# Convolution of an H3 block beside attention: one channel or two in each strip of 32 PSUM rows

## The chip, the core and the metric

The kernel runs on one core of one Trainium2 chip. The core has five engines that run side by side and meet only at semaphores: TensorE (PE: matrix products, with its weight loads shown as PEld), VectorE (DVE), ScalarE (ACT), GpSimd (POOL) and SyncE (SP, which here only issues DMA transfers). Matrix products end in PSUM, which has 128 rows (partitions) and 8 banks of 512 fp32 columns. The metric is the device time of one execution in microseconds (us).

## The reference

Two blocks are computed independently and their outputs stand side by side in the last dimension. S is 2048, D is 512, all tensors are bf16.

```python
# block A: attention, 32 heads of 16
q, k, v = split(x @ wqkv)
a = softmax(q @ k.T * 16 ** -0.5) @ v        # per head
a = merge_heads(a) @ wo
# block B: a short and a long causal convolution per channel
kv = shift_conv(k, shift_k) * v              # 4 taps along S
y = long_conv(kv, ssm_k) + kv * ssm_D        # filter as long as S, per channel
b = q * y
out = concatenate([a, b], -1)                # (1, 2048, 1024)
```

The reference does the long convolution with FFTs. The kernel does it directly, as matrix products with a Toeplitz matrix of each channel's filter.

## The kernel before

**Attention sets the pace.** The 2048 x 2048 scores of 32 heads are cut into 2048 blocks of 128 keys x 512 queries. A step (number `T`) handles 2 or 3 blocks: `emit_qk` (L776) issues the score products into as many PSUM banks, ACT takes the exponential of all of them in one instruction (L794) of 1024 or 1536 columns into the ring `PT`, and two steps later `emit_pv` multiplies by the values (L862). In part of the steps with three blocks one block is not given to ACT: `exp_on_dve` (L808) computes it on DVE in four passes (L813, L822 twice, L823), with one linear pass on POOL (L289) between the first and the second. So a block can be moved from ACT to DVE, which makes one ACT instruction 1024 columns instead of 1536 and adds four DVE passes.

**The convolution fills PE's gaps.** Time is cut into 16 blocks of 128 (`NB` is 16). For a channel, output block t is the sum over lags n of a 128 x 128 Toeplitz matrix times input block t - n. The tile `KV` (`[128, channel/4, block, channel%4]`) holds the gated input, blocks in reverse order. For a lag, the stationary operand is `KV` of one channel, blocks n to 15 (16 - n columns), and the moving operand is 128 columns of the channel's filter windows `WR`. Four channels run at once, one in each strip of 32 PSUM rows (`tile_position=(0, 32 * c)`), and such a group of four is a `qd`: 128 of them, each with 16 lags, 8192 matmuls in all (`conv_lags`, L977 to L1006, the matmul at L988). A channel's result fills rows 0 to 15 of its strip and 128 columns of the bank `BGB`; rows 16 to 31 stay unused. Four `qd`s fill the bank's 512 columns, then DVE copies the bank to one half of `YB` (L1004), which frees the bank. When both halves are full, `conv_turn` (L1009) transposes them with eight matmuls (L1015) into a bank of the attention's ring, and one DVE product with the gate `QN` (L1030) gives 32 finished channels. So 32 copies and 16 turns are made.

**The filter's way.** `kz_turn` (L625) reverses the 512 filter rows into `KZS`, four neighbouring channels in each partition. `kz_store` (L630) writes `KZS` to the scratch `kz_scratch` in HBM with one DMA, row d of the scratch being channel d. `load_wr` (L965) then reads for row d, 128 times overlapping, `128 x 2048` windows into a ring of 14 slots, on SP's queue; the first loads wait for the store. Behind the store on SP's queue stand loads of `B_v` and `B_k` for the gated input (`load_kv`, L418).

**What sets the order.** Each engine executes in order, and that order is made when the program is built: the code keeps its own estimate of each engine's clock (`Eng.t`, `Mm`). `commit_one` (L292) picks the next DVE job by its due time. `form` (L1246) decides at each step whether a third block goes to DVE, by the DVE work that is still open (`DVE_OPEN`), and whether a side task (`next_unit`: projections, a turn, an output product) takes the third bank. `emit_lags` (L1124) puts convolution lags into the time that PE has before the next scores are due, and stops at a new bank fill while `BGB` isn't free. `keep_active` (L1102) adds products with zeros to an open sum where little PE work is planned. A change of any job's count therefore rearranges the program.

Of the kernel before, what the change touches and what calls it, by code (L numbers as in the profile page):

```python
# [24 lines left out]
C = 512  # L25
NB = S // 128
# [145 lines left out]
def bass_concat_heads__mha_block__ssm_conv_h3__prompt_kernel(  # L172
# [24 lines left out]
    def sb(name, shape, dt=BF16):  # L197
        return enter(nc.sbuf_tensor(name, shape, dt))
# [5 lines left out]
    VAF = sb("VAF", [128, KT, VROW])  # L204
    PT = sb("PT", [128, R_PT, 3 * QB])
    WR = sb("WR", [128, R_W, S])
    KV = sb("KV", [128, C // 4, NB, 4])
    QN = sb("QN", [128, NB, 256])
    WQ = sb("WQ", [128, 4, D])
    MSK = sb("MSK", [128, 2, 4], FP32)  # L210
# [10 lines left out]
    EI = sb("EI", [128, 4, QB], INT32)  # L221
    EM = sb("EM", [128, 2, QB], FP32)
    ZER = sb("ZER", [128, 128])
    XL = KV[:, :, :, :].rearrange("p q t r -> p (q t r)").rearrange("p (t d) -> p t d", t=NB)
    XH = EI[:, :, :].rearrange("p i f -> p (i f)").bitcast(BF16).rearrange("p (t d) -> p t d", t=8)

    def xn(t):
# [130 lines left out]
    def full(n, k):  # L358
        return [("full", 0, n)] * k

    def dma(eng, dsem, outp, inp, deps=(), transpose=False):
        h = dsem.add()

        def fn(e):
            f = e.dma_start_transpose if transpose else e.dma_start
            f(outp, inp).then_inc(dsem.sem, 16)  # L366
        eng.op(fn, deps, inc=False)
        return h
# [89 lines left out]
    vones = VAF[:, :, 0:H * VW].rearrange("p k (h e) -> p k h e", e=VW)  # L458
    pool.op(lambda e: e.memset(vones[:, :, :, DH:VW], 1.0))
    h_vaf1 = pool.op(lambda e: e.memset(VAF[:, :, H * VW:VROW], 1.0))  # L460
    h_zer = pool.op(lambda e: e.memset(ZER[:, :], 0.0))
    h_kz0 = pool.op(lambda e: e.memset(KZS[:, :, S:S + PAD], 0.0))
    pool.op(lambda e: e.wait_ge(*h_xn[3]), inc=False)
# [165 lines left out]

    def kz_store():  # L630
        h = dve_op(lambda e: e.tensor_tensor(KZS[:, :, S - 1:S], KZS[:, :, S - 1:S], DSS, ALU.add), [h_kzt[0]], 100.0)
        h_kzw[0] = dma(sp, d_kzw, kz_ap.rearrange("(p c) m -> p c m", c=4), KZS, [h, h_kz0])

    kv_pieces += [lambda c=c: kz_turn(c) for c in range(4)] + [lambda: (kz_store(), load_kv(5, h_kzt[0]))]
    for j in range(7, -1, -1):
# [326 lines left out]
    h_wr, h_wrfree, h_qn = {}, {}, {}  # L962
    h_yb, h_yb_in = {}, {}

    def load_wr(d, deps=()):  # L965
        r = d % R_W
        deps = [h_kzw[0], *deps] if d < R_W else [h_wrfree[d - R_W]]
        if d < R_W:
            line[0] += 1350.0
        src = bass.AP(tensor=kz_ap.tensor, offset=kz_ap[d, 0].offset, ap=[[1, 128], [1, S]])  # L970
        h_wr[d] = dma(sp, d_wr[r], WR[:, r, :], src, deps)
# [3 lines left out]
                      q2[128 * t0:128 * t1, 256 * i:256 * i + 256].rearrange("(t p) d -> p t d", p=128), deps)  # L975

    def conv_lags(qd, n0, n1):  # L977
        kk = qd % 8
        deps = [h_wr[4 * qd + c] for c in range(4)] + [h_kvc[0]]
        if kk % 4 == 0 and n0 == 0:  # L980
            deps.append(bank_free[BGB])

        def fn(e):
            ins = None
            for n in range(n0, n1):
                for c in range(4):
                    d = 4 * qd + c
                    ins = e.matmul(PS[32 * c:32 * c + NB - n, BGB, 128 * (kk % 4):128 * (kk % 4) + 128],  # L988
                                   lhsT=KV[:, qd, n:NB, c],
                                   rhs=WR[:, d % R_W, 128 * (NB - 1 - n):128 * (NB - n)],  # L990
                                   start=(n == 0), stop=(n == NB - 1), tile_position=(0, 32 * c))
            return ins
        h = pe_op(fn, deps, [("col", c, 128) for n in range(n0, n1) for c in range(4)])
        if n1 == NB:
            for c in range(4):
                h_wrfree[4 * qd + c] = h
                if 4 * qd + c + R_W < C:
                    load_wr(4 * qd + c + R_W)
            if kk % 4 == 3:
                half = kk // 4  # L1000
                src = PS[:, BGB, :]
                src = bass.AP(tensor=src.tensor, offset=PS[:, BGB, 127:128].offset,
                              ap=[src.ap[0], [128, 4], [-1, 128]])
                bank_free[BGB] = dve_job(lambda e: e.tensor_copy(YB[:, half, :].rearrange("p (k i) -> p k i", k=4), src),  # L1004
                                         [h, (lambda: h_yb.get(qd // 8 - 1, WAIT)) if qd >= 8 else None])
                h_yb_in[qd // 4] = bank_free[BGB]  # L1006
        return h

    def conv_turn(b, bank, slack):  # L1009
        pbf = PS[:, bank, :].bitcast(BF16)  # L1010

        def fn(e):
            ins = None
            for k in range(8):
                ins = e.transpose(pbf[:, 128 * k:128 * k + 128], YB[:, k // 4, 128 * (k % 4):128 * (k % 4) + 128],  # L1015
                                  IDN[:, :])
            return ins
        h = pe_op(fn, [bank_free[bank], h_yb_in[2 * b], h_yb_in[2 * b + 1], h_idn], full(128, 8))
        h_yb[b] = h
        sl = b // 8  # L1020
        yv = pbf.rearrange("p (c j) -> p c j", j=32)[:, :, 0:NB].rearrange("p c j -> p j c")
        yv = bass.AP(tensor=yv.tensor, offset=pbf[:, NB - 1:NB].offset, ap=[yv.ap[0], [-1, NB], [32, CHB]])
        qv = QN[:, :, CHB * (b % 8):CHB * (b % 8) + CHB]

        def store(hh):
            dst = out2[:, D + 256 * sl:D + 256 * (sl + 1)].rearrange("(t p) c -> p t c", p=128)
            ho = dma(pool, d_outB[0], dst, QN[:, :, :], [hh])
            if sl == 0:
                dve_later.append((len(chunks) + 14, lambda: load_qn(1, [ho], 0, NB)))
        bank_free[bank] = dve_job(lambda e: e.tensor_tensor(qv, yv, qv, ALU.mult), [h, lambda: h_qn.get(sl, WAIT)],  # L1030
                                  slack=slack, then=store if b % 8 == 7 else None)
# [26 lines left out]
    def next_unit(T):  # L1058
        st = state
        found = []  # L1060
        if st["u"] < len(units):
            n, u = units[st["u"]]
            free = st["started"] and flow["nxt"] >= 4 * KT * (int(n) - 2 * NG + 2) if n >= NG else True
            if free and steps_to(n) < 40:
                found.append((steps_to(n) - 16, "u", u))
        if st["turn"] > st["turned"] and at_job(h_yb_in[2 * st["turned"] + 1]) + 45.0 <= pe.t:
            found.append((4.0 - st["qd"] % 4 * 4 + 8, "turn", st["turned"]))
        if st["op"] < len(later_op) and at_job(h_otn.get(later_op[st["op"]][0] * 4 + 3, WAIT)) + 45.0 <= pe.t:
            u = later_op[st["op"]]
            found.append((steps_to((u[0] + 2) * NG) - 40, "op", u))  # L1070
        return min(found, key=lambda x: x[0]) if found else None
# [52 lines left out]
    def emit_lags(T):  # L1124
        st = state
        if T in tail_mm:
            assert st["qd"] == C // 4 and st["turned"] == C // 32 and st["op"] == len(later_op), (T, st)
            for t, j in tail_mm[T]:
                op_mm(NQB - 1, t, j, j + 1, tail_banks[t])
            keep_tail(T)  # L1130
            return
        if st["qd"] == C // 4:
            if flow["NT"] is None or T < flow["NT"] - 12:
                bank_free[BGB] = pe_op(keep_busy, [bank_free[BGB]], full(512, 2))
            else:
                keep_tail(T)
            return
        if not st["started"]:
            fill(max(max(Mm.tile), pe.t), at_of(h_exp[T]) - PE_SLACK)
            st["now"] = at_of(h_exp[T])  # L1140
            return
        limit = at_of(h_exp[T]) - PE_SLACK
        now = at_of(h_exp[T])
        ahead = [(st["wr"][i] + 1500.0 - now) / (NB * (i - st["qd"]) - st["lag"]) for i in range(st["qd"] + 1, len(st["wr"]))]
        st["lags"] = min(st["lags"] + (now - st["now"]) / max([PACE] + ahead), 2.0 * LAGS)
        st["now"] = now
        lags = LAGS
        while st["qd"] < C // 4:
            t = max(max(Mm.tile), pe.t)
            advance(t)  # L1150
            n0 = st["lag"]
            if n0 == 0 and (st["wr"][st["qd"]] + 1000.0 > t or st["qd"] % 4 == 0 and at_job(bank_free[BGB]) > t):
                if st["qd"] % 4 == 0 and lags == LAGS:
                    fill(t, limit)
                break
            k = min(lags, int(st["lags"]), NB - n0, int((limit - t) / LAG_NS))
            if k < 1:
                break
            lags -= k
            st["lags"] -= k  # L1160
            conv_lags(st["qd"], n0, n0 + k)
            st["lag"] = (n0 + k) % NB
            if n0 + k == NB:
                st["qd"] += 1
                st["dma"] = max(st["dma"], max(Mm.tile) + 2500.0) + DMA_NS
                st["wr"].append(st["dma"])
                st["turn"] = st["qd"] // 8
# [227 lines left out]
```

## Time and profile before

| | us |
|---|---|
| median of 3 runs (lowest, highest) | 847.8 (844.84, 854.87) |
| the profiled execution, its own time | 846.45 |
| its span in the profile | 844.7 |
| ACT, DVE, PE busy | 820.3, 799.2, 714.4 |

The span runs from the first to the last instruction that the profile shows; the rest of the profiled execution's time, 1.75 us, lies around it. In the views an instruction is named by its line, its engine, its operation and its tiles. PE's busy time overlaps with itself (several matmuls in flight), so its sum says little of how full PE is; ACT and DVE execute one after the other, and their busy shares can be read as they stand.

### The profile page before, as it was taken

How to read it: one execution, taken by the hardware profiler on the slowest of the kernel's cores; microseconds unless marked ns; L12 is line 12 of the kernel's file. 1: busy time of each engine (PE TensorE's matmuls, PEld its weight loads, DVE VectorE, ACT ScalarE, POOL GpSimd, SP SyncE). 2: the span in 40 equal slices, each digit the busy share in tenths (PEclk: the TensorE clock that was granted, in tenths of full speed). 3: DMA queues.
4: the chain of work that ended last, by engine and by line, in shares of the span. 5: the costliest groups of instructions: out<-in, count | busy, mean ns of one | idle time of the engine just before them, and what ended most of it. 6: DMA issues, size and time to landing. Idle time of an engine off the chain costs nothing.

```text
span 844.7 us, 30021 instructions
## 1 busy us (share of the span) xinstructions
PE 714.4 (85%) x13191; PEld 308.0 (36%) x13238; DVE 799.2 (95%) x1346; ACT 820.3 (97%) x732; POOL 287.9 (34%) x318
## 2 busy tenths in 40 slices
PE   8988888888888888888888888888788888888897
PEld 3322333433344333343333333333334433334332
DVE  3998899999999999999999999999999999999996
ACT  6998999999999999999999999999999999999997
POOL 3232233333433333333333423333333333333331
PEclk9999999999999999999999999999999999999999
DMA  9978699999999999999999999999999999999810
GB/s 314 314 255 298 211 410 343 370 408 402 391 375 371 373 410 365 390 385 390 365 376 365 321 408 407 408 374 373 357 378 390 363 400 404 364 381 396 320 52 25
DMA packets 88435, 295.69 MB, mean 350 GB/s; under 512 B 11125, under 2 KB 19314, under 8 KB 87922
## 3 DMA queue, kind: packets, MB, share of 16 engines
q1 hardware_dynamic: 82386, 280.00, 87.6%
q0 software_dynamic: 3776, 12.58, 4.4%
q8 instruction: 105, 1.72, 0.8%
q10 hardware_dynamic: 2144, 1.18, 0.5%
q14 instruction: 24, 0.20, 0.1%
HBM read 287.31 MB, written 6.42 MB: 348 GB/s over the span
## 4 chain that ended last, share of the span: by engine, by line
ACT 59%; DVE 25%; PE 9%; issue 2%; DMA 2%; POOL 1%; SPq 1%; ACTq 0%; DVEq 0%
ACT PT L794 59%; DVE PTD L823 5%; DVE EI L813 5%; DVE EM L822 5%; DVE WKV L822 4%; PE PS L787 3%; PE PS L862 2%; DMA WR<-in_B_ssm_D_dram 2%; SPq L366 1%; DVE DT L888 1%; PE PS L988 1%; DVE YB L1004 1%; DVE QT L540 1%; PE PS L936 1%; DVE OUTA L948 1%
## 5 line engine op out<-in xcount | busy, mean ns | idle before, releaser
L794 ACT ACTIVATE PT<-PS 128x1024 bf16<-128x1024 f32 (+1 forms) x726 | 816.7, 1337 | 12.9 <-PE PS L787 11.1
L787 PE MATMUL PS<-QT,KTo 32*128 32x512 bf16 x2048 | 287.9, 385 | 110.4 <-ACT PT L794 91.2
L988 PE MATMUL PS<-WR,KV 128*7 128x128 bf16 (+15 forms) x8192 | 252.8, 220 | 3.4 <-issue 3.2
L289 POOL TENSOR_SCALAR EM<-EI 128x512 f32<-128x512 uint16 x129 | 125.2, 970 | 235.6 <-DVE WKV L822 104.1
L988 PEld LDWEIGHTS PS<-WR,KV 128*7 128x7 bf16 (+15 forms) x8192 | 169.5, 87 | 83.7 <-issue 42.4
L289 POOL TENSOR_SCALAR WKV<-EI 128x512 f32<-128x512 uint16 x128 | 125.0, 977 | 199.9 <-DVE EM L822 86.1
L862 PE MATMUL PS<-PT,VAF 128*32 128x512 bf16 x1791 | 187.8, 392 | 2.0 <-issue 0.8
L813 DVE TENSOR_SCALAR EI<-PS 128x512 int32<-128x512 f32 x257 | 176.0, 685 | 4.1 <-PE PS L787 3.9
L822 DVE SCALAR_TENSOR_TENSOR EM<-EM 128x512 f32<-128x512 f32 x258 | 173.9, 686 | 2.7 <-POOL EM L289 2.5
L787 PEld LDWEIGHTS PS<-QT,KTo 32*128 32x128 bf16 x2048 | 72.0, 91 | 273.2 <-ACT PT L794 213.4
L822 DVE SCALAR_TENSOR_TENSOR WKV<-WKV 128x512 f32<-128x512 f32 x256 | 170.7, 689 | 0.5 <-POOL WKV L289 0.4
L823 DVE SCALAR_TENSOR_TENSOR PTD<-EI,EM 128x512 uint16<-128x512 int32 x129 | 88.6, 689 | 0.4
L823 DVE SCALAR_TENSOR_TENSOR PTD<-EI,WKV 128x512 uint16<-128x512 int32 x128 | 87.5, 687 | 0.4
L862 PEld LDWEIGHTS PS<-PT,VAF 128*32 128x32 bf16 x1791 | 47.6, 93 | 108.2 <-issue 97.3
L862 PE MATMUL PS<-PTD,VAF 128*32 128x512 bf16 x257 | 79.3, 389 | 0.4
L1112 PE MATMUL PS<-IDN,ZER 128*32 128x512 bf16 x424 | 46.6, 381 | 0.1
L888 DVE STREAM_TRANSPOSE DT<-PS 128x512 f32<-128x512 f32 x31 | 22.2, 716 | 7.5 <-PE PS L862 7.0
L862 PEld LDWEIGHTS PS<-PTD,VAF 128*32 128x32 bf16 x257 | 19.8, 95 | 17.4 <-DVE PTD L823 6.7
L540 DVE TENSOR_TENSOR QT<-PS,MSK 128x1024 bf16<-128x1024 f32 x15 | 18.4, 1224 | 4.5 <-PE PS L505 4.3
L1004 DVE CAST YB<-PS 128x512 bf16<-128x512 f32 x32 | 22.0, 687 | 0.4 <-PE PS L988 0.2
L366 POOL DMA_DIRECT2D WR<-in_B_k_dram x15 | 11.0, 741 | 23.3 <-DVE KV L616 14.8
L519 PE MATMUL PS<-WKV,xT 128*128 128x512 bf16 x58 | 17.8, 383 | 1.0 <-issue 0.8
(79 smaller groups left out, 292.6 us busy)
## 6 DMA issues: line engine op xcount, KB each, us to landing
WR<-kz_scratch SPq DMA_DIRECT2D x512, 512.0 KB, 8.0
WR<-in_B_k_dram POOLq DMA_DIRECT2D x15, 256.0 KB, 7.6
kz_scratch<-WR SPq DMA_DIRECT2D x1, 2176.0 KB, 8.6
out_dram<-QN POOLq DMA_DIRECT2D x2, 1024.0 KB, 8.0
QT<-in_B_k_dram POOLq DMA_DIRECT2D x7, 256.0 KB, 8.8
out_dram<-OUTA POOLq DMA_DIRECT2D x12, 128.0 KB, 6.4
WR<-in_B_v_dram SPq DMA_DIRECT2D x5, 256.0 KB, 9.1
WR<-in_B_k_dram SPq DMA_DIRECT2D x5, 256.0 KB, 10.6
```

What stands on the lines that cost most here:

```text
L289: q.h = pool.op(lambda e: e.tensor_scalar(UB[m % len(UB)], f, PA, PB, ALU.mult, ALU.add), [h, fx.h, free], cost=Beside((h[0], h[1] + 1)))
L540: hh = dve_job(lambda e: e.tensor_tensor(QT[:, qb % 2, 2 * o:2 * o + 2, :], src, MSK[:, :, 0:1].broadcast_to([128, 2, QB]), ALU.mult), [h, ...
L787: ins = e.matmul(PS[:, bank, :], lhsT=KTo[32 * s:32 * s + 32, g // 2, kt * 128:(kt + 1) * 128], rhs=QT[32 * s:32 * s + 32, qb % 2, g, :], ...
L794: h_exp[T] = act.op(lambda e: e.activation(PT[:, T % R_PT, 0:n * QB], PS[:, banks[0]:banks[0] + n, :].rearrange("p b f -> p (b f)"), ACT.E ...
L813: h_fix[i] = job(lambda e: e.tensor_scalar(ei, PS[:, bank, :], FIX_LO, FIX_ADD, ALU.max, ALU.add), [h, h_pair.get(i - 4)], 692.0, end)
L822: js.append(job(lambda e, c=c: e.scalar_tensor_tensor(u, u, c, u, ALU.add, ALU.mult), [js[-1]], 693.0, due + 700.0 * (len(js) - 3)))
L823: js.append(job(lambda e: e.scalar_tensor_tensor(PTD[:, i % 4, :].bitcast(UINT16), ei, 2.0 ** -9, u, ALU.mult, ALU.add), [js[2], (lambda: ...
L862: ins = e.matmul(PS[32 * s:32 * s + 32, pvb(qb * NG + g), :], lhsT=VAF[:, kt, h * VW:h * VW + 32], rhs=rhs, start=first[b], stop=last[b], ...
L888: h_t = dve_job(lambda e: e.transpose(out=dt, in_=PS[:, pvb(n), :]), [h, h_mult.get(n - 2 if n == 2 else n - 1) if n != 1 else None], 717. ...
L988: ins = e.matmul(PS[32 * c:32 * c + NB - n, BGB, 128 * (kk % 4):128 * (kk % 4) + 128], lhsT=KV[:, qd, n:NB, c], rhs=WR[:, d % R_W, 128 * ( ...
L1004: bank_free[BGB] = dve_job(lambda e: e.tensor_copy(YB[:, half, :].rearrange("p (k i) -> p k i", k=4), src), [h, (lambda: h_yb.get(qd // 8 ...
L1112: ins = e.matmul(PS[32 * s:32 * s + 32, pvb(n), :], lhsT=ZER[:, 0:32], rhs=IDN[:, :].rearrange("p (a f) -> p a f", a=1).broadcast_to([128, ...
```

## The change

Two channels share a strip: one in rows 16 to 31, the other in rows 0 to 15. The strip's first channel gets a stationary operand of 32 - n columns: the channel's own blocks and, ahead of them, the 16 blocks that lie before them in the tile, those of the channel four lower (for the first channels, 64 columns of zeros, which are added to the tile, now `KVP`, and set by POOL). Its product puts the channel's result into rows 16 to 31 and unwanted sums into rows 0 to 15. Then the second channel's products, 16 - n columns as before, start afresh in rows 0 to 15 and overwrite these. So eight `qd`s fill a bank where four did; a bank holds 32 channels; `YB`'s halves become two whole buffers, and a turn takes four transposes of one of them. `chan(d)` says which channel the d-th filter row belongs to, and `kz_store` writes the rows to the scratch in that order, with four DMAs (one for each of the four rows of a partition), so that `load_wr` still reads row d of the scratch.

```diff
-    KV = sb("KV", [128, C // 4, NB, 4])
+    KVP = sb("KVP", [128, 4 * NB + C * NB])
+    KV = KVP[:, 4 * NB:4 * NB + C * NB].rearrange("p (q t r) -> p q t r", t=NB, r=4)
...
+    h_kvp = pool.op(lambda e: e.memset(KVP[:, 0:4 * NB], 0.0))
...
     def kz_store():
...
-        h_kzw[0] = dma(sp, d_kzw, kz_ap.rearrange("(p c) m -> p c m", c=4), KZS, [h, h_kz0])
+        rows = kz_ap.rearrange("(o e h j) m -> o h e j m", e=2, h=2, j=2)
+        for i in range(4):
+            h_kzw[0] = dma(sp, d_kzw, rows[:, :, 1 - i % 2, i // 2, :], KZS[:, i, :], [h, h_kz0])
...
+    def chan(d):
+        return 8 * (d // 8) + 2 * (d % 4) + 1 - d % 8 // 4
...
     def conv_lags(qd, n0, n1):
-        kk = qd % 8
-        deps = [h_wr[4 * qd + c] for c in range(4)] + [h_kvc[0]]
-        if kk % 4 == 0 and n0 == 0:
+        kk = qd // 2 % 4
+        m = 2 - qd % 2
+        deps = [h_wr[4 * qd + c] for c in range(4)] + [h_kvc[0], h_kvp]
+        if qd % 8 == 0 and n0 == 0:
             deps.append(bank_free[BGB])
...
-                    ins = e.matmul(PS[32 * c:32 * c + NB - n, BGB, 128 * (kk % 4):128 * (kk % 4) + 128],
-                                   lhsT=KV[:, qd, n:NB, c],
+                    ch = chan(d)
+                    o = 4 * NB * (ch // 4 + 2 - m) + 4 * n + ch % 4
+                    ins = e.matmul(PS[32 * c:32 * c + m * NB - n, BGB, 128 * kk:128 * kk + 128],
+                                   lhsT=KVP[:, o:o + 4 * (m * NB - n) - 3:4],
                                    rhs=WR[:, d % R_W, 128 * (NB - 1 - n):128 * (NB - n)],
                                    start=(n == 0), stop=(n == NB - 1), tile_position=(0, 32 * c))
...
-            if kk % 4 == 3:
-                half = kk // 4
+            if qd % 8 == 7:
+                half = qd // 8 % 2
...
     def conv_turn(b, bank, slack):
...
-            for k in range(8):
-                ins = e.transpose(pbf[:, 128 * k:128 * k + 128], YB[:, k // 4, 128 * (k % 4):128 * (k % 4) + 128],
-                                  IDN[:, :])
+            for k in range(4):
+                ins = e.transpose(pbf[:, 128 * k:128 * k + 128], YB[:, b % 2, 128 * k:128 * k + 128], IDN[:, :])
...
-        yv = bass.AP(tensor=yv.tensor, offset=pbf[:, NB - 1:NB].offset, ap=[yv.ap[0], [-1, NB], [32, CHB]])
+        yv = bass.AP(tensor=pbf.tensor, offset=pbf[:, NB - 1:NB].offset, ap=[pbf.ap[0], [-1, NB], [NB, CHB]])
```

The remaining lines follow from these: `next_unit` asks for one full buffer instead of two halves, and `emit_lags` treats every eighth `qd` as a new bank fill instead of every fourth.

More of the change, by code (lines that the diff above doesn't have):

```diff
@@ L223, in bass_concat_heads__mha_block__ssm_conv_h3__prompt_kernel @@
     ZER = sb("ZER", [128, 128])
-    XL = KV[:, :, :, :].rearrange("p q t r -> p (q t r)").rearrange("p (t d) -> p t d", t=NB)
+    XL = KVP[:, 4 * NB:4 * NB + C * NB].rearrange("p (t d) -> p t d", t=NB)
     XH = EI[:, :, :].rearrange("p i f -> p (i f)").bitcast(BF16).rearrange("p (t d) -> p t d", t=8)
@@ L1004, in conv_lags @@
                 bank_free[BGB] = dve_job(lambda e: e.tensor_copy(YB[:, half, :].rearrange("p (k i) -> p k i", k=4), src),
-                                         [h, (lambda: h_yb.get(qd // 8 - 1, WAIT)) if qd >= 8 else None])
-                h_yb_in[qd // 4] = bank_free[BGB]
+                                         [h, (lambda: h_yb.get(qd // 8 - 2, WAIT)) if qd >= 16 else None])
+                h_yb_in[qd // 8] = bank_free[BGB]
         return h
@@ L1013, in fn @@
             ins = None
-            for k in range(8):
-                ins = e.transpose(pbf[:, 128 * k:128 * k + 128], YB[:, k // 4, 128 * (k % 4):128 * (k % 4) + 128],
-                                  IDN[:, :])
+            for k in range(4):
+                ins = e.transpose(pbf[:, 128 * k:128 * k + 128], YB[:, b % 2, 128 * k:128 * k + 128], IDN[:, :])
             return ins
-        h = pe_op(fn, [bank_free[bank], h_yb_in[2 * b], h_yb_in[2 * b + 1], h_idn], full(128, 8))
+        h = pe_op(fn, [bank_free[bank], h_yb_in[b], h_idn], full(128, 4))
         h_yb[b] = h
         sl = b // 8
-        yv = pbf.rearrange("p (c j) -> p c j", j=32)[:, :, 0:NB].rearrange("p c j -> p j c")
-        yv = bass.AP(tensor=yv.tensor, offset=pbf[:, NB - 1:NB].offset, ap=[yv.ap[0], [-1, NB], [32, CHB]])
+        yv = bass.AP(tensor=pbf.tensor, offset=pbf[:, NB - 1:NB].offset, ap=[pbf.ap[0], [-1, NB], [NB, CHB]])
         qv = QN[:, :, CHB * (b % 8):CHB * (b % 8) + CHB]
@@ L1065, in next_unit @@
                 found.append((steps_to(n) - 16, "u", u))
-        if st["turn"] > st["turned"] and at_job(h_yb_in[2 * st["turned"] + 1]) + 45.0 <= pe.t:
-            found.append((4.0 - st["qd"] % 4 * 4 + 8, "turn", st["turned"]))
+        if st["turn"] > st["turned"] and at_job(h_yb_in[st["turned"]]) + 45.0 <= pe.t:
+            found.append((12.0 - st["qd"] % 8 * 2, "turn", st["turned"]))
         if st["op"] < len(later_op) and at_job(h_otn.get(later_op[st["op"]][0] * 4 + 3, WAIT)) + 45.0 <= pe.t:
@@ L1151, in emit_lags @@
             n0 = st["lag"]
-            if n0 == 0 and (st["wr"][st["qd"]] + 1000.0 > t or st["qd"] % 4 == 0 and at_job(bank_free[BGB]) > t):
-                if st["qd"] % 4 == 0 and lags == LAGS:
+            if n0 == 0 and (st["wr"][st["qd"]] + 1000.0 > t or st["qd"] % 8 == 0 and at_job(bank_free[BGB]) > t):
+                if st["qd"] % 8 == 0 and lags == LAGS:
                     fill(t, limit)
```

## The prediction

> **What bounds the kernel now.** I read the page first (busy times, then the chain that ended last), then the groups of instructions with shapes kept apart, then the waits, and last the order in time around the filter's store and around one piece of the convolution.
>
> ```profile
> span 844.7 us, 30021 instructions
> PE 714.4 (85%) x13191; PEld 308.0 (36%) x13238; DVE 799.2 (95%) x1346; ACT 820.3 (97%) x732; POOL 287.9 (34%) x318
> ...
> ACT 59%; DVE 25%; PE 9%; issue 2%; DMA 2%; POOL 1%; SPq 1%; ACTq 0%; DVEq 0%
> ACT PT L794 59%; DVE PTD L823 5%; DVE EI L813 5%; DVE EM L822 5%; DVE WKV L822 4%; PE PS L787 3%; PE PS L862 2%; DMA WR<-in_B_ssm_D_dram 2%; SPq L366 1%; DVE DT L888 1%; PE PS L988 1%; DVE YB L1004 1%; DVE QT L540 1%; PE PS L936 1%; DVE OUTA L948 1%
> ```
>
> ACT is busy for 97% of the span and DVE for 95%. The chain runs through ACT for 59% and through DVE for 25%: the two share the exponentials and are loaded about equally. PE's share of the chain is 9%. So a change on PE counts only where it makes ACT wait, and work taken from DVE counts by what it takes off ACT.
>
> ```profile
> L794 ACT ACTIVATE PT<-PS 128x1536 bf16<-128x1536 f32 x339 | 518.3, 1577 | 5.2 <-PE PS L787 4.6
> L794 ACT ACTIVATE PT<-PS 128x1024 bf16<-128x1024 f32 x387 | 422.1, 1128 | 7.8 <-PE PS L787 6.5
> L813 DVE TENSOR_SCALAR EI<-PS 128x512 int32<-128x512 f32 x257 | 176.0, 685 | 4.1 <-PE PS L787 3.9
> L822 DVE SCALAR_TENSOR_TENSOR EM<-EM 128x512 f32<-128x512 f32 x258 | 173.9, 686 | 2.7 <-POOL EM L289 2.5
> L823 DVE SCALAR_TENSOR_TENSOR PTD<-EI,EM 128x512 uint16<-128x512 int32 x129 | 88.6, 689 | 0.4
> L1004 DVE CAST YB<-PS 128x512 bf16<-128x512 f32 x32 | 22.0, 687 | 0.4 <-PE PS L988 0.2
> ...
> L1015 PE MATMUL PS<-IDN,YB 128*128 128x128 bf16 x128 | 9.9, 220 | 0.4 <-DVE EI L813 0.4
> ```
>
> These rows (busy total, mean of one, idle time before) price both engines. ACT waits 5.2 + 7.8 = 13.0 us in all between its exponentials, little beside 844.7. A block of 512 columns that leaves an ACT instruction of 1536 makes it one of 1024: by busy time 518.3/339 - 422.1/387 = 1529 - 1091 = 438 ns, by the mean durations 1577 - 1128 = 449 ns. The same block on DVE is four passes of 685, 686, 686 and 689 ns, 2.75 us.
>
> ```profile
> PEld PS L787 <- ACT PT L794: 213.4, 448, 2.3
> PE PS L787 <- ACT PT L794: 91.2, 212, 2.1
> ACT PT L794 <- PE PS L787: 11.1, 24, 1.3
> POOL WR L366 <- DMA EI<-in_A_x_dram: 8.5, 1, 8.5
> ```
>
> In the waits (total us, times, longest) PE stands before the score products because ACT hasn't freed their banks: the matmuls 212 times for 91.2 us, 0.43 us each, their weight loads for 213.4 us. The reverse happens 24 times for 11.1 us.
>
> **Copies on DVE.** 16 of the 32 copies of the bank go. Their price is 16 x 687 ns = 11.0 us of DVE. The time isn't left free: the build order of the changed program has 261 blocks on DVE instead of 257, and on ACT 391 instructions of 1024 columns and 335 of 1536, still 726. Four more blocks cost DVE 4 x 2.75 = 11.0 us, exactly what was freed. DVE therefore comes out level, and ACT loses 4 x 0.438 = 1.75 us (1.80 by the other price). POOL gets four linear passes more, and is idle most of the time (34%). This is the one term on the path: -1.75 us.
>
> **Transposes and fills on PE.** 64 of 128 transposes go, half of 9.9 us busy, and the build order has 28 fewer of the products with zeros. This is PE time; it is worth nothing where PE then waits longer for ACT. In the 16 turn steps four transposes fewer let the following scores start earlier, but only a step in which ACT was waiting for PE turns that into time. I take 0; the most it can be is the 11.1 us of the wait row, and turns stand in 16 of 726 steps, so in truth a few tenths of a us.
>
> **The convolution's matmuls.** Their number stays 8192, with 128 moving columns each; 4096 of them now have 17 to 32 stationary columns instead of 1 to 16, which no convolution row of this trace shows. The nearest rows:
>
> ```profile
> L988 PE MATMUL PS<-WR,KV 128*16 128x128 bf16 x512 | 37.5, 222 | 0.0
> L988 PE MATMUL PS<-WR,KV 128*1 128x128 bf16 x512 | 37.2, 219 | 0.0
> L988 PEld LDWEIGHTS PS<-WR,KV 128*16 128x16 bf16 x512 | 16.2, 93 | 7.8 <-issue 4.7
> L988 PEld LDWEIGHTS PS<-WR,KV 128*1 128x1 bf16 x512 | 14.8, 82 | 4.7 <-issue 2.7
> L862 PEld LDWEIGHTS PS<-PT,VAF 128*32 128x32 bf16 x1791 | 47.6, 93 | 108.2 <-issue 97.3
> ...
> 402.32 0.51 PE L988 MATMUL PS<-WR,KV 128*16 128x128 bf16 x24
> ```
>
> The matmul lasts 219 to 222 ns at 1 and at 16 columns. The load grows from 82 to 93 ns, 0.73 ns a column, but the 32-column load of the attention's value product takes 93 ns too. In the piece at 402.32, 24 matmuls (six lags of four strips) take 0.51 us with their last one's 0.22 in it, so a lag starts every (0.51 - 0.22)/5 = 0.06 us; the loads of 0.09 us must therefore lie beside earlier matmuls. Bounds: from 0 (the 93 ns row) to 16 x 0.73 = 11.7 ns for each wide load. With four strips loading side by side the upper end is 1024 x 11.7 ns = 12 us of PE, one after another 48 us. I take 0, because the value product's row is for the very shape in question, and PE's wait for ACT covers the 12 us: spread over the steps it is under 0.02 us each against 0.43.
>
> [...]
>
> **Waits around the bank.** A bank is now filled by eight groups, so PE stands before a busy `BGB` 16 times instead of 32. That can only help; it is hidden behind PE's other waits, 0. The new wait of the first convolution products for the zeros in `KVP` is for one small POOL memset at the start; behind it POOL stands 8.5 us for the input anyway (last row above), and the gated input that the same products wait for is made much later: 0. The copy that starts a turn comes from one job instead of two; the turns stay at 16.
>
> **The store of the filter rows and SP's queue.** One DMA becomes four, with pieces of 2176 x 2 bytes instead of four times that.
>
> ```profile
> 27.18 0.34 SPq L366 DMA_DIRECT2D kz_scratch<-WR  x1
> 27.56 0.43 SPq L366 DMA_DIRECT2D QN<-in_B_v_dram  x1
> 28.04 0.97 SPq L366 DMA_DIRECT2D QT<-in_B_k_dram  x1
> ...
> 44.36 0.95 SPq L366 DMA_DIRECT2D WR<-kz_scratch  x2
> ...
> 43.60 1.29 DVE L596 TENSOR_TENSOR QT<-QT,WR 128x1024 bf16<-128x1024 bf16 x2
> ...
> WR<-kz_scratch SPq DMA_DIRECT2D x512, 512.0 KB, 8.0
> ...
> kz_scratch<-WR SPq DMA_DIRECT2D x1, 2176.0 KB, 8.6
> ...
> QT<-in_B_k_dram SPq DMA_DIRECT2D x2, 256.0 KB, 7.9
> ```
>
> Three more issues of 0.34 us move the two loads behind them on SP by 1.0 us. The later of them is issued at 28.04 and lands 7.9 us later, at 36; its first reader on DVE (the tap at 43.60) comes 7.6 us after that. So 1 us is hidden; past 7.6 us DVE would wait. The store landed 8.6 us after its issue, at 35.8, and its first reader on SP is issued at 44.36. Four stores lie between 8.6 us, as before, and four times the 8.0 us of a load of about that size (32 us, landing at about 60); the second would hold SP's queue for some 16 us, the gated input with it. I take the first, the row for the same bytes. 0, and a few us in the range.
>
> **Sum.** -1.75 us against the profiled execution, whose own time is 846.45 (span 844.7 and 1.75 around it): 844.7. The median of the three runs shown is 847.8, 1.35 above the profiled one, so for a median I set 846.0.
>
> **The rivals.** First, DVE may be the true limit. For it: 25% of the chain is DVE's, and the copy alone has 1% of it, some 8 us, so half of that, 4 us, could come off. If all 16 copies lay on the path and the four new blocks cost nothing extra, it would be 11.0 + 1.75 = 12.8 us, 835. Against it: the freed passes are refilled one for one, so each chain through DVE keeps its length. 840 to 835, chance 0.11 for at least the step below 839.
>
> Second, slower: new waits of ACT for scores. The edits shift due times, so the DVE jobs and side tasks of nearly the whole program stand in another order. The present order leaves ACT 24 waits on score products, 11.1 us; an order whose evacuations come late more often would have more of them. Twice as many give 847.8 - 1.75 + 11.1 = 857. The point from which it decides: about 10 us of added waits, when the result leaves the band of 1%. For it: ACT and DVE have no slack left. Against it: the same rules place both orders. Chance 0.08.
>
> Third, slower as well: the wide loads aren't covered and run one after another, 48 us more on PE. PE's loads wait for ACT in 448 of 726 steps, so in the other 278 (38%) the added time reaches ACT: 0.38 x 48 = 18 us, 864. It decides when a wide lag costs more than the spare 0.43 us of a step. [...] Chance 0.04.
>
> Fourth, nothing of the exchange arrives, because ACT's wait grows by what its work shrinks: 847.8, inside the same band.
>
> **How the numbers follow.** The forecast has 0.77: ACT's waits in a new order may be some 5 us less or more than now (half of 11.1), so 841 to 851 on its own, and the three runs shown spread over 10 us. The first rival reaches down to 835, the second up to 857. With a tenth left out on either side: 837 to 855. One per cent is 8.5 us, about what a measurement here can tell from no change: faster than 839.3 needs most of the first rival, 0.11; slower than 856.3 needs the second or third, 0.12; between them 0.77.
>
> **What would show it.** Right: 16 copies to `YB` of about 687 ns and 64 transposes; 261 first passes on DVE; ACT busy near 818.5 and DVE near 799; loads of 17 to 32 columns at 93 to 97 ns, and pieces of 24 matmuls still 0.51 us; the four stores landing before about 38 us; the wait of ACT for the score products between 6 and 16 us. Wrong: DVE's share of the chain falling with a span under 838 (first rival); that wait at 20 us or more (second); wide lags starting over 0.07 us apart with PE's own wait for ACT gone (third); DVE standing for a load between 43 and 60 us (the store).

## The result and the profile after

The changed kernel took 845.09 us (median of 20 runs, 841.61 to 848.2), the kernel before 848.58 (20 runs, 844.55 to 854.87). The ratio, which is that of the means, is 0.9953, with a 95% interval of 0.9932 to 0.9974: 4.0 us less, between 2.2 and 5.8. That is inside the range of the prediction and inside its band of 1%, on the side that was forecast, and more than the 1.75 us of its sum.

The profiled execution of the changed kernel is one of its longest, 848.2 us, and its span is longer than that of before. So the spans can't be compared, but the work can. From the page:

```profile
span 846.4 us, 29917 instructions
PE 719.9 (85%) x13144; PEld 310.1 (37%) x13144; DVE 798.4 (94%) x1346; ACT 819.2 (97%) x732; POOL 290.6 (34%) x323
...
ACT 71%; PE 13%; DVE 12%; issue 2%; DMA 1%; POOL 1%; ACTq 0%; DVEq 0%
```

From the groups by line with shapes kept apart (busy us, mean ns of one, idle us before):

```profile
L798 ACT ACTIVATE PT<-PS 128x1536 bf16<-128x1536 f32 x335 | 510.0, 1566 | 9.6 <-PE PS L791 9.4
L798 ACT ACTIVATE PT<-PS 128x1024 bf16<-128x1024 f32 x391 | 422.6, 1124 | 6.8 <-PE PS L791 5.4
L817 DVE TENSOR_SCALAR EI<-PS 128x512 int32<-128x512 f32 x261 | 177.3, 679 | 7.0 <-PE PS L791 6.7
...
L1014 DVE CAST YB<-PS 128x512 bf16<-128x512 f32 x16 | 10.9, 682 | 0.0
```

16 copies are left and 261 blocks go to DVE. DVE's 1346 instructions are as many as before (798.4 us busy against 799.2): the copies were replaced one for one by exponential passes. ACT's busy time falls from 820.3 to 819.2, although ACT waits more in this execution: 9.6 + 6.8 = 16.4 us between exponentials, 13.0 before. The waits say the same:

```profile
ACT PT L798 <- PE PS L791: 14.8, 30, 1.8
```

It was 11.1 us in 24 waits. The longest of them, at 475 us, leads to what the prediction had no term for. Windows of 3.4 us each, from the trace of the kernel before and then of the changed one (length; busy us of PE, PEld, DVE, ACT and POOL, each with its count; then the clock granted to TensorE, the DMA engines' share, GB/s):

```profile
405.80:409.20 3.40, 2.06 (x46) 0.81 (x47) 2.61 (x5) 3.40 (x4) 1.99 (x2) 1.00 1.02 406
409.20:412.60 3.40, 3.40 (x46) 1.48 (x49) 2.55 (x5) 2.47 (x3) 0.00 (x0) 0.51 0.99 374
```

```profile
352.70:356.10 3.40, 2.12 (x45) 0.77 (x43) 3.40 (x7) 3.40 (x4) 2.22 (x3) 1.00 1.03 410
356.10:359.50 3.40, 3.40 (x51) 1.93 (x50) 2.46 (x5) 3.00 (x3) 0.76 (x1) 0.50 1.03 410
359.50:362.90 3.40, 2.63 (x57) 1.22 (x55) 3.17 (x6) 2.77 (x3) 0.00 (x0) 1.00 1.03 408
472.20:475.60 3.40, 1.13 (x33) 0.49 (x25) 3.40 (x7) 1.65 (x3) 1.00 (x1) 1.00 1.02 405
475.60:479.00 3.40, 3.40 (x45) 1.22 (x38) 1.40 (x3) 3.12 (x3) 1.00 (x1) 0.50 1.03 416
```

PE was busy here for 2.06, 2.12 and 1.13 us of a stretch of 3.4 us (its average is 85%, 2.9 us), and the clock granted to it in the next 3.4 us was 0.51, 0.50 and 0.50. In the first two cases ACT is full in the stretch before and falls to 2.47 and 3.00 us in the slow one. In the third ACT loses its time before the slow stretch: PE stops for 2.27 us in the middle of a group of lags, ACT then waits 1.75 us for scores and does 1.65 us of work, and 3.12 at half clock. So a stretch at half clock marks lost time, and not all of that time is lost at half clock.

Little PE work wasn't always followed by half clock. In the kernel before, 2.12 us of it were followed by a clock of 1.00:

```profile
600.38:603.79 3.41, 2.12 (x42) 1.03 (x46) 2.45 (x5) 2.10 (x3) 1.19 (x2) 1.00 1.01 371
603.79:607.20 3.41, 2.98 (x74) 1.32 (x69) 3.41 (x6) 3.41 (x4) 0.93 (x1) 1.00 0.98 389
```

Over the 14 traces of this case, without the first 60 and the last 20 us of each, all 20 windows at full clock with under 2.0 us of PE work were followed by one at half clock, 24 of the 158 with 2.0 to 2.4 us, and none of the 2886 with more. The trace of the kernel before and that of the changed one have 2 of 2, 5 of 23 and none of 412 of these.

Away from head and tail the profiled execution of before has two slow windows (409.2 and 716.4), that of the changed kernel five (356.1, 475.6, 605.3, 615.5, 793.0), each 3.41 us long, which is why its mean granted clock is 0.989 against 0.995; its longer span goes with them.

What stood ahead of some of the slow windows is in the traces. The stop of 2.27 us in the order in time, and a transfer of 16 KB (0.02 MB) that starts at 472.32 on the queue that the profile names instruction (view of the DMA queues from 472.3 to 473.4):

```profile
474.77 0.22 PE L998 MATMUL PS<-WR,KVP 128*8 128x128 bf16 x1 [2.27 <-issue]
```

```profile
q8 instruction: 1, 0.02, 5.6%
```

The median distance of these transfers is 7.0 us in the kernel before and 7.1 in the changed one. In the 14 traces, from 60 us on and without the last 25 us, PE stops 45 times for 0.7 us or more without waiting for anything that the profile shows (`issue`), and every one of these stops ends 2.2 to 2.7 us after such a transfer has started. No run changes these transfers, so whether PE stands because of them was not shown. Such a stop lies in the stretch before four of the seven slow windows named above (409.2, 475.6, 605.3 and 615.5); what left PE with little work before the other three stays open.

Since every run comes with its mean granted clock, times can be compared at the same clock. The 95 runs of the kernel before that were taken beside the experiments (three more, of 861.93, 867.09 and 1408.64 us, count as slow and are left out here and below) scatter about a straight line over the clock: 5.9 us more for each per cent lost (correlation 0.92), 844.7 us at a clock of 0.997. The changed kernel's 20 runs: 4.2 us for each per cent, 843.1 at 0.997. Without a line: the 29 runs of before with a clock of 0.995 or more average 844.97 us, the seven such runs of the changed kernel 843.22, which is 1.75 us less.

### The profile page after: what moved, and what is told of

Same layout as the page of the kernel before. It is cut to its first block, busy times and chain, and to the rows that moved or that the text cites. A ratio compares the mean times of both kernels' runs of the same rounds, so it can differ in the third digit from the quotient of the medians.

```text
span 846.4 us, 29917 instructions
## 1 busy us (share of the span) xinstructions
PE 719.9 (85%) x13144; PEld 310.1 (37%) x13144; DVE 798.4 (94%) x1346; ACT 819.2 (97%) x732; POOL 290.6 (34%) x323
## 4 chain that ended last, share of the span: by engine, by line
ACT 71%; PE 13%; DVE 12%; issue 2%; DMA 1%; POOL 1%; ACTq 0%; DVEq 0%
ACT PT L798 71%; PE PS L791 5%; PE PS L866 2%; DVE PTD L827 2%; DVE EM L826 2%; DVE EI L817 2%; PE PS L521 2%; DVE WKV L826 2%; PE PS L998 1%; PE PS L940 1%; DMA WKV<-in_A_wqkv_dram 1%; DVE OUTA L952 1%; PE PS L507 1%; PE PS L514 1%; DMA QT<-in_B_k_dram 1%
## 5 line engine op out<-in xcount | busy, mean ns | idle before, releaser
L798 ACT ACTIVATE PT<-PS 128x1024 bf16<-128x1024 f32 (+1 forms) x726 | 815.6, 1328 | 16.4 <-PE PS L791 14.8
L998 PE MATMUL PS<-WR,KVP 128*30 128x128 bf16 (+15 forms) x8192 | 258.7, 222 | 4.7 <-issue 4.2
L998 PEld LDWEIGHTS PS<-WR,KVP 128*29 128x29 bf16 (+15 forms) x8192 | 178.2, 95 | 79.7 <-issue 40.4
L290 POOL TENSOR_SCALAR EM<-EI 128x512 f32<-128x512 uint16 x131 | 126.9, 969 | 224.3 <-DVE WKV L826 114.8
L826 DVE SCALAR_TENSOR_TENSOR WKV<-WKV 128x512 f32<-128x512 f32 x260 | 173.1, 682 | 2.0 <-POOL WKV L290 1.8
L1120 PE MATMUL PS<-IDN,ZER 128*32 128x512 bf16 x396 | 44.1, 382 | 0.0
L367 POOL DMA_DIRECT2D out_dram<-OUTA x12 | 7.1, 593 | 34.8 <-DVE OUTA L952 34.8
```

The lines of the kernel that those rows point to most:

```text
L290: q.h = pool.op(lambda e: e.tensor_scalar(UB[m % len(UB)], f, PA, PB, ALU.mult, ALU.add), [h, fx.h, free], cost=Beside((h[0], h[1] + 1)))
L798: h_exp[T] = act.op(lambda e: e.activation(PT[:, T % R_PT, 0:n * QB], PS[:, banks[0]:banks[0] + n, :].rearrange("p b f -> p (b f)"), ACT.E ...
L826: js.append(job(lambda e, c=c: e.scalar_tensor_tensor(u, u, c, u, ALU.add, ALU.mult), [js[-1]], 693.0, due + 700.0 * (len(js) - 3)))
L998: ins = e.matmul(PS[32 * c:32 * c + m * NB - n, BGB, 128 * kk:128 * kk + 128], lhsT=KVP[:, o:o + 4 * (m * NB - n) - 3:4], rhs=WR[:, d % R_ ...
L1120: ins = e.matmul(PS[32 * s:32 * s + 32, pvb(n), :], lhsT=ZER[:, 0:32], rhs=IDN[:, :].rearrange("p (a f) -> p a f", a=1).broadcast_to([128, ...
```

## The experiments

Each was run 6 to 12 times beside the kernel before (29 to 35 runs in each of three sessions). The ratios are not quotients of the medians beside them. The last two columns are the mean granted clock of the runs, and the time that a least-squares line through the runs of that kernel gives at a clock of 0.997 (the scatter about the lines is 0.4 to 1.4 us; the standard error of a value is 0.2 to 1.0 us, and 1.8 us for e8 with its six runs).

```
                                median   ratio (95%)               clock   at 0.997
kernel before, session of e1-e4   846.92                           0.993
               session of e5-e8   847.40                           0.991
               session of e9-e12  848.96                           0.990
               all 95 runs                                         0.992   844.7
changed kernel                  845.09   0.9953 (0.9932-0.9974)    0.993   843.1
e1  wide loads                  845.12   0.9990 (0.9963-1.0017)    0.993   844.4
e2  four stores                 848.06   1.0004 (0.9973-1.0035)    0.992   844.3
e3  copies back                 852.01   1.0076 (1.0046-1.0106)    0.984   846.4
e4  257 blocks                  846.15   0.9990 (0.9969-1.0011)    0.994   845.2
e5  changed, 5200               851.57   1.0036 (1.0000-1.0072)    0.990   847.9
e6  before, 5200                848.60   1.0018 (0.9986-1.0050)    0.993   847.0
e7  changed, 5600               845.08   0.9970 (0.9941-1.0000)    0.994   844.0
e8  before, 5600                858.46   1.0116 (1.0078-1.0154)    0.987   855.3
e9  before, 340 ns              848.95   1.0008 (0.9975-1.0040)    0.990   845.4
e10 changed, 340 ns             850.35   1.0024 (0.9993-1.0054)    0.985   843.7
e11 before, 355 ns              850.36   1.0021 (0.9993-1.0049)    0.987   845.1
e12 changed, 355 ns             843.07   0.9923 (0.9897-0.9949)    0.995   842.1
```

**Wide loads alone.** On the kernel before, with `KVP` as in the change:

```diff
-PS[32 * c:32 * c + NB - n, BGB, ...], lhsT=KV[:, qd, n:NB, c],
+PS[32 * c:32 * c + 2 * NB - n, BGB, ...],
+lhsT=KVP[:, 4 * NB * qd + 4 * n + c:4 * NB * qd + 4 * n + c + 4 * (2 * NB - n) - 3:4],
-offset=pbf[:, NB - 1:NB].offset
+offset=pbf[:, 2 * NB - 1:2 * NB].offset
```

> The kernel before, with all 8192 stationary operands of the convolution 17 to 32 columns wide (the result in rows 16 to 31 of each strip, unwanted sums below them that nothing reads); one channel a strip, 32 copies, 257 blocks on DVE, the same order. Wide loads cost nothing: ratio to the kernel before 1.000, within 0.002. If each wide load cost 11.7 ns with four strips at once, 2048 lags are 24 us of PE, of which the 38% of steps without a spare pass on 9 us: ratio 1.011.

The ratio is 0.999, and 844.4 at the same clock. Its groups:

```profile
L990 PE MATMUL PS<-WR,KVP 128*32 128x128 bf16 x512 | 37.9, 225 | 0.0
L990 PE MATMUL PS<-WR,KVP 128*17 128x128 bf16 x512 | 37.3, 221 | 0.0
L990 PEld LDWEIGHTS PS<-WR,KVP 128*32 128x32 bf16 x512 | 18.6, 108 | 8.0 <-issue 5.0
L990 PEld LDWEIGHTS PS<-WR,KVP 128*17 128x17 bf16 x512 | 16.8, 95 | 4.5 <-issue 2.7
```

The loads did become longer, 95 to 108 ns, and the matmuls behind them did not. ACT's instructions come in the same order as before from first to last. Twice as many wide loads as the change has cost nothing that can be measured.

**Four stores alone.** On the kernel before:

```diff
-h_kzw[0] = dma(sp, d_kzw, kz_ap.rearrange("(p c) m -> p c m", c=4), KZS, [h, h_kz0])
+rows = kz_ap.rearrange("(p c) m -> p c m", c=4)
+for i in range(4):
+    h_kzw[0] = dma(sp, d_kzw, rows[:, i, :], KZS[:, i, :], [h, h_kz0])
```

> The kernel before, with the scratch written by four DMAs instead of one, rows in their old order. In the changed kernel SP needed 4.0 us for the four issues instead of 0.34, so the two loads behind them start about 3.5 us later; with 7.6 us to spare before their first reader that is hidden: ratio 1.000, within 0.002. If DVE waits for them after all: up to 3 us, 1.0035, and DVE idle before the taps near 43 us.

Order in time on SP and on DVE in this run (start us, duration us):

```profile
27.35 2.23 SPq L366 DMA_DIRECT2D kz_scratch<-WR  x4
29.62 1.19 SPq L366 DMA_DIRECT2D QN<-in_B_v_dram  x1
30.85 1.61 SPq L366 DMA_DIRECT2D QT<-in_B_k_dram  x1
...
44.38 0.95 SPq L366 DMA_DIRECT2D WR<-kz_scratch  x2
```

```profile
43.76 1.28 DVE L596 TENSOR_TENSOR QT<-QT,WR 128x1024 bf16<-128x1024 bf16 x2
```

The four issues take 2.23 us (4.0 in the changed kernel's trace) where one took 0.34, and the second load behind them starts at 30.85 instead of 28.04. The tap that reads it starts at 43.76, without a wait, where it started at 43.60 before. Hidden, as expected: ratio 1.0004. (The 7.6 us to spare are a misreading; see the store below.)

**The copies given back.** On the changed kernel each bank is copied twice, with the second copy freeing the bank:

```diff
-bank_free[BGB] = dve_job(lambda e: e.tensor_copy(YB[:, half, :]..., src), [h, ...])
+first = dve_job(lambda e: e.tensor_copy(YB[:, half, :]..., src), [h, ...])
+bank_free[BGB] = dve_job(lambda e: e.tensor_copy(YB[:, half, :]..., src), [first])
```

> The changed kernel with each of its 16 bank copies made twice, so DVE has 32 copies again; the build order then holds 256 blocks on DVE and 340 wide exponentials. If the gain is the exchange of copies for exponentials, it is gone: ratio to the kernel before 1.000 to 1.002. If the gain comes from something else (fewer bank fills and transposes on PE, another order), it stays: 0.995 to 0.997.

The gain is gone, as the exchange demands, and more: 1.0076, above the expected 1.000 to 1.002, with no run below 849. Part of the excess goes with the clock, 0.984. In the profiled execution the half clock sets in before the convolution has begun, and lasts for four windows:

```profile
68.90:72.30 3.40, 1.99 (x16) 0.60 (x16) 3.37 (x6) 2.45 (x3) 0.00 (x0) 1.00 1.02 408
72.30:75.70 3.40, 3.40 (x16) 0.53 (x12) 2.99 (x6) 2.08 (x3) 2.10 (x1) 0.50 0.61 246
75.70:79.10 3.40, 3.40 (x14) 0.52 (x12) 0.33 (x1) 2.05 (x2) 3.10 (x6) 0.50 0.50 133
79.10:82.50 3.40, 3.40 (x14) 0.75 (x12) 3.05 (x6) 2.05 (x2) 0.38 (x1) 0.50 0.81 253
82.50:86.00 3.50, 3.17 (x14) 0.78 (x13) 1.83 (x5) 1.90 (x2) 0.00 (x0) 0.50 0.01 2
86.00:89.40 3.40, 3.40 (x21) 0.93 (x20) 3.24 (x9) 3.26 (x4) 0.00 (x0) 1.00 0.44 133
```

PE is busy all the time in three of the four by the profile, so its busy share alone did not bring the full clock back there. Up to that point this kernel's order is the changed kernel's, which kept the full clock there after 2.15 us of PE work; the kernel before at 340 ns and the changed kernel at 5600 fell there too, at 73.2 and 72.8. At a clock of 0.997 the line gives 846.4, 1.7 us above the kernel before, of which one block fewer on DVE explains 0.4. The rest is open, with a standard error of 1.0 us, so e3 is no clean measure of the exchange.

**The freed time not refilled.** On the changed kernel the third block is let to DVE at a limited rate:

```diff
-if T >= flow["half"] and T >= T_DVE and load < DVE_OPEN and flow["left"] > DVE_END:
+if T >= flow["half"] and T >= T_DVE and load < DVE_OPEN and flow["left"] > DVE_END and len(on_dve) < 4 + 0.398 * (T - T_DVE):
```

> The changed kernel with the third block's way to DVE limited so that 257 blocks go there, as before the change: the 11 us of DVE are free and not refilled. Exchange alone: ACT has its old work, ratio to the kernel before 0.999 to 1.000. If looser work on DVE is worth something by itself (fewer late evacuations, so fewer waits of ACT and PE): 0.995 to 0.998.

```profile
PE 710.2 (84%) x13110; PEld 309.8 (37%) x13156; DVE 794.2 (94%) x1330; ACT 819.7 (97%) x732; POOL 287.2 (34%) x319
```

Everything of the change is in this kernel except the four blocks, and its order on ACT and DVE is the changed kernel's up to 536 us. DVE executes 1330 instructions instead of 1346 and is 5.0 us less busy than before the change, and the ratio is 0.999 (0.9969 to 1.0011); at the same clock 845.2, 0.5 above the kernel before and 2.1 above the changed kernel. Free time on DVE, half the transposes and half the bank fills are worth nothing that these runs can tell from zero.

**More work against the half clock.** `ACTIVE`, the planned work in a window below which products with zeros are added, raised in both kernels (`ACTIVE = 4800.0` to `5200.0`, then `5600.0`):

> The changed kernel with the threshold below which products with zeros are added on PE raised from 4800 to 5200 (748 such matmuls instead of 396; still 261 blocks on DVE). If the spread of the runs comes from stretches in which PE's clock is granted at half after little work on PE, the mean granted clock of the runs rises from 0.993 to 0.996 or more and the median comes near 843.1, where the changed kernel's runs lie at 0.997: ratio to the kernel before about 0.994. If the clock does not follow PE's work, or the zeros delay the scores: clock unchanged, ratio 0.996 or above.

> The kernel before with the same threshold of 5200 (732 products with zeros instead of 424; 258 blocks on DVE). Clock theory: granted clock 0.996 or more, ratio to the kernel before 0.997 (its runs lie at 844.9 at a clock of 0.997 against a median of 847). Otherwise 1.000 or above. The difference to the changed kernel at the same threshold should be the exchange alone, three blocks, 1.3 to 1.8 us.

> The changed kernel with the threshold at 5600 (964 products with zeros, 260 blocks on DVE). Clock theory: granted clock 0.997 or more, no further gain than at 5200 beyond 1 us, less one block (0.4 us): ratio 0.994. If the zeros get in the way of scores and values: slower than at 5200 by 2 us or more.

> The kernel before with the threshold at 5600 (984 products with zeros, 257 blocks on DVE). Clock theory: ratio 0.997, and 1.3 us above the changed kernel at 5600 (three blocks). Otherwise 1.000 or above.

The expectation failed. The granted clock stayed between 0.987 and 0.994, and three of the four became slower at the same clock too (847.9, 847.0 and 855.3 against 843.1 and 844.7). In the last one the page and the waits show how much fuller PE is:

```profile
PE 755.4 (88%) x13802; PEld 317.9 (37%) x13802; DVE 802.0 (94%) x1346; ACT 823.5 (96%) x732; POOL 286.2 (33%) x318
```

```profile
PE PS L787 <- ACT PT L794: 55.2, 139, 0.9
```

PE's spare time before the scores, 91.2 us in the kernel before, is down to 55.2. Its profile also has ten of the stops behind an instruction transfer, 11.6 us, against four, 3.6 us, in the kernel before; the fastest kernel, the changed one at 355 ns, has none of 0.7 us or more. Where an added product is planned isn't where a stretch turns out empty: in the changed kernel's window at 472.2 it was such a stop, in the middle of a group of lags. Why the changed kernel at 5600 did not suffer (844.0), with four stops, 4.8 us, is open.

**Other orders.** The planned distance of lags (`PACE = 350.0`) set to 340 and to 355 in both kernels. The counts of blocks stay at 257 and 261; the order changes from the convolution's start on.

> The kernel before with convolution lags spread at 340 ns instead of 350 (257 blocks on DVE as before, 404 products with zeros, another order from the convolution's start on). If the order alone is worth little, ratio to the kernel before 1.000, within 0.002. If it is worth as much as the runs with more zeros suggest, anywhere from 0.997 to 1.006.

> The changed kernel at 340 ns (261 blocks, 424 products with zeros). Exchange: 1.75 us under the kernel before at the same 340 ns, compared at the same granted clock. If only the order made the changed kernel faster, the pair differs by anything, in either direction.

> The kernel before at 355 ns (257 blocks, 432 products with zeros). As at 340: 1.000 within 0.002 if the order is worth little, 0.997 to 1.006 if it is worth more.

> The changed kernel at 355 ns (261 blocks, 472 products with zeros). Exchange: 1.75 us under the kernel before at 355 ns at the same granted clock; the mean over the three pairs (340, 350, 355) is then near 1.75. If the order decides, the three differences spread by 3 us or more and their mean says little.

By medians the three pairs disagree: the changed kernel is 1.4 us slower at 340, 3.5 faster at 350 and 7.3 faster at 355. At a clock of 0.997 they agree within their errors: 1.7, 1.6 and 3.0 us faster (each good to some 0.5 to 0.9 us), 2.1 on average. The differences between the medians go with the clock: at 340 the changed kernel has 0.985 against 0.990, at 355 0.995 against 0.987. The changed kernel at 355 ns, 0.9923 (0.9897 to 0.9949), beats both kernels of the case.

## Why the prediction was right, and where its size was off

- **The exchange** (-1.75 us, the only term on the path) is what the change is worth at the same clock: 1.75 us between the averages of runs at 0.995 or more, 1.6 by the lines, 2.1 over three orders. Without the four blocks nothing is left (e4); with the copies back nothing is left either, but e3 lies 1.3 us higher than the exchange explains. The term held: 261 blocks as built, and about 0.4 us for each. One price under it was too high. Contrary to what stands under the profile before, instructions of DVE overlap, and those of ACT too, so that a mean duration isn't what one more of them costs. DVE in the kernel before:

```profile
299.98 0.68 DVE L822 SCALAR_TENSOR_TENSOR EM<-EM 128x512 f32<-128x512 f32 x1
300.57 0.69 DVE L822 SCALAR_TENSOR_TENSOR WKV<-WKV 128x512 f32<-128x512 f32 x1
```

  They start 0.60 us apart, so the 16 copies cost nearer 9.6 us than 11.0, and so do the 16 passes that took their place; the exchange one for one isn't touched. ACT's exponentials, where one follows on another, start 0.90 us apart after 1024 columns and 1.33 after 1536 (medians of the same trace): 0.43 us for a block, as taken.
- **What the sum lacked** is the time that goes with the clock. The medians differ by 3.5 us and the means by 4.0, so some 2 us of the result aren't the exchange. At 5.9 us for each per cent, a difference of 0.3 to 0.4 per cent in the mean clock of the two sets of runs would make that up. This part is argued and not shown: the clock of the 20 runs of the kernel before that stood beside the changed one isn't known, only that of 95 others, 0.992 on average (0.990 to 0.993 by session) against the changed kernel's 0.993. Those 20 runs average 848.97 us and the 95 others 847.94, so 1.0 us of the 4.0 lies in which runs of the kernel before stood beside it. The changed kernel's smaller loss per cent (4.2) would add to it.
- **Luck.** That 845.09 came out so near to the 846.0 of the forecast is partly luck: the median of three runs that it starts from is 0.8 us too low, and the gain that it takes off is too small. The sign of the medians depends on the order, too: with lags at 340 ns the same change is 1.4 us slower by medians.
- **The transposes, the bank waits and the fills** at 0: right within the error, e4 has all of them and no gain.
- **The wide loads** at 0: right in what they cost, wrong in the reason. I took the 93 ns of the value product's 32-column load over the growth from 1 to 16 columns, and expected 93 to 97 ns. The changed kernel's own rows:

```profile
L998 PEld LDWEIGHTS PS<-WR,KVP 128*32 128x32 bf16 x256 | 9.2, 108 | 5.7 <-issue 4.5
...
L998 PEld LDWEIGHTS PS<-WR,KVP 128*1 128x1 bf16 x256 | 7.6, 83 | 3.8 <-issue 1.8
```

  From 1 to 32 columns the load grows by 25 ns, 0.81 ns a column. The upper bound of my estimate, 16 x 0.73 = 11.7 ns on top of the 93 ns at 16 columns, 105 in all, was the better guide to the load. What kept it off the path was the other reason given: the loads lie beside earlier matmuls. Why the value product's 32 columns load in 93 ns stays open: its columns lie side by side, as do the 128 of the scores (91 ns in the kernel before), the convolution's four elements apart, and no run varies that alone. A piece of 24 matmuls takes as long as before:

```profile
104.24 0.51 PE L998 MATMUL PS<-WR,KVP 128*27 128x128 bf16 x24
```

- **The store** at 0: right in the time, wrong in the reading. The 7.9 us from issue to landing is the median of two loads; the one in question, issued at 28.04, took longer, and landed at 40.0 (view of the tile `QT` on SP's queue):

```profile
DMA to landing us min/median/max: 11.9/11.9/11.9
```

  So it had 3.6 us to spare before the tap at 43.60, not 7.6. In the changed kernel the four issues took 4.0 us and not 4 x 0.34, so that it was issued 3.9 us later, at 31.98, more than it had to spare. It was hidden because it landed no later, at 39.6:

```profile
DMA to landing us min/median/max: 7.6/7.6/7.6
```

  The last of the four stores had landed at 37.2, as forecast.
- **The rivals.** DVE as the true limit falls with e4: 5 us less work on DVE, and no time. Its share of the chain went from 25% to 12% in a longer execution, so that share wasn't worth the 8 us read into it. Waits from a new order, the second rival, are real in both directions (an order alone moved medians by up to 7 us), but they show mainly in the clock: at 0.997 the three orders lie within 0.7 us for the kernel before and 1.6 us for the changed one. The lines can't tell what is lost at half clock from what is lost in the stretch before it. Uncovered loads fall with e1.

## What to carry to other kernels

When two engines share the same work and both are full, time freed on one of them is worth only what it lets the other hand over: here 16 copies of DVE, some 10 us, bought some 1.7 us of ACT. Before reading a difference of half a per cent as the edit's, compare the runs at the same granted clock, and try the same edit in another order of the program.

## What the runs showed of the hardware

- In the 14 traces all 20 windows of 3.4 us at full clock with under 2.0 us of PE work were followed by one at half clock, 24 of the 158 with 2.0 to 2.4 us, and none of the 2886 with more (first 60 and last 20 us left out). Over the runs a per cent of mean granted clock went with 3.5 to 7.6 us, by kernel (5.9 in the 95 runs of the kernel before), and most of the spread of one kernel's runs went with it (correlation 0.92 in those 95).
- In e3 the half clock lasted from 72.3 to 86.0 us, four windows of 3.4 or 3.5 us in which PE was busy for 3.17 to 3.40 us by the profile and ACT did 1.90 to 2.08 us of work.
- All 45 stops of PE of 0.7 us or more in which it waits for nothing that the profile shows (first 60 and last 25 us left out) end 2.2 to 2.7 us after the start of a 16 KB transfer on the queue that the profile names instruction; the longest lasts 2.27 us.
- Four DMA issues in a row on SP took 2.23 us in e2 and 4.0 us in the changed kernel, against 0.34 for one DMA of the same bytes.
